# Second gate's row, e' group order, last q projection and third MLP pair's rows moved in a one-core attention and MLP block

## The chip, the cores and the metric

The kernel runs on one core of a Trainium2 chip. The metric is the time of one execution on the device in microseconds (us); lower is better. The engines are PE (matrix products, with weight loads PEld), DVE (vector), ACT (scalar), POOL (GpSimd) and SP (it issues DMAs; ACT and POOL issue some as well). They run in parallel, each through its own instructions in order.

## The reference

One transformer block on 2048 tokens of width 640 in float32. Both halves are modulated by a condition `c`.

```python
mod = (silu(c) @ w_mod).reshape(1, 6, 1, -1)
sa, ca, ga, sb, cb, gb = six rows of mod
h = layernorm(x) * (1 + ca) + sa
x = x + ga * A(h)          # linear attention, 32 heads of 20
h = layernorm(x) * (1 + cb) + sb
x = x + gb * B(h)          # (relu(h @ w1 + b1) ** 2) @ w2 + b2, 1728 hidden columns

# A: q, k, v = h @ wqkv; pq, pk = per-head products with w_phi
phi = concat(softmax(p), softmax(-p))
o   = phi_q @ (phi_k^T v) / (phi_q @ sum(phi_k) + 1e-6)
A   = o @ wo
```

## The kernel before

Tokens are taken in 16 tiles of 128 rows, or 8 pairs. Products are made in float32 by splitting each operand into a high and a low part (three products each: high-high, high-low, low-high; `mm(three(...))`, line 78). The low part is a subtraction on DVE (`lo`, line 88).

The first stage, to about 250 us, makes k and v for all tiles, q for most, and sums phi_k^T v in PSUM. In the same stage the modulation rows are made. The second gate (row 5 of `mod`) ends as a column form `MT[5]`, in a row buffer of the pool tag `s1`; `mod_sum(5, gate_b)` reduces it to `gate_b`, 128x5, on DVE (line 310). `spread_row` (lines 328, 329) then writes `gate_b` to DRAM as 640 single elements and reads it back broadcast to all 128 partitions as `gb_b`; both DMAs are on SP. The first gate is treated the same way earlier (`gate_a`, `ga_b`).

The second stage, from about 252 to 389 us, is written out by hand for PE, DVE, ACT and POOL (lines 768 to 1216); the order of SP's DMAs is left to the scheduler there. Its first lines project the last q tiles (`do_q`) and treat pair 0. Then a loop runs over the pairs, `for j in range(NB)`. For a tile t:

- `e_prod(t)` on DVE multiplies phi_q by the sum of phi_k (`scr`) and reduces by head (`dn`); POOL finishes the denominators; `e_recip` and `e_scale` on DVE give the scaled features `ezb` (e').
- `tr_e(j, groups)` transposes the scaled features of a pair on PE in six groups (`te`): groups 0 to 4 with four transposes, group 5 with two. Each group goes into one of three PSUM banks in turn and is evicted by ACT into an `ept` row (five buffers).
- `num(j)` makes the numerators (`numa`, `numb`, `numc`), groups 0 to 5 in order; `num_hi` evicts the high part on ACT (`ot`, line 950). `num_lo` makes the low part: for pairs 0 and 1 PE subtracts the high part in PSUM (line 961) and ACT copies (line 964); later DVE subtracts (`ot`, line 88).
- `do_wo` makes the product with `wo` (`pwo`); ACT evicts it to `at` (line 982, two buffers) and issues its store (line 984).

In pair j of the loop the groups for pair j+1 are transposed in two batches, at two of three places (`te(0)` behind the first product with `wo`, `te(1)` behind the second, `te(2)` behind the third). The last q tiles' feature chains (`q_chain`, `exps`, `q_sums`) are spread over pairs 1, 3 and 5. Pair 3 ends with `mod_sum` and `spread_row` of the second gate. Pair 5 makes the first pair's new residual rows (`add_x(0, 0, 1)`: x plus attention, stored to DRAM as X1) and `bb = b2s * gb_b`, where `b2s` is a row of `s1` that holds b2 on all partitions. `p_load`, `p_hi` and `p_lo` load and split the MLP's weight rows (row buffers of `s1`).

The third stage is the MLP, pair by pair: `up` (seven groups n of two 128-column pieces), relu on ACT (line 1250), square on DVE (line 1251), splits `ra` and `rs`, and the product with w2. From pair 2 on a scheme with fewer products is used, with sums of blocks of the hidden values (`sums`, line 1265) and prepared combinations of w2, which come from DRAM through four ring buffers (`ring_a`, `ring_b`, `ring_c`, fetched by POOL at line 1360 as soon as a buffer is free). Between the products, `layer(j+1, at)` prepares the next pair's layer norm: loads, `add_x` (line 1080, with the store of X1 at line 1081), the statistics (`ln_pieces`, ACT lines 1494 and 1499 and small steps on POOL) and the transposes. The dictionaries `LN_AT...` say at which half group each step stands; `LN_AT2` is for the pair prepared during pair 2, where SP's order is written by hand as well. `residual` loads the old X1 rows (`xr`).

Of the kernel before, what the change touches and what calls it, by code (L numbers as in the profile page):

```python
# [11 lines left out]
AF = mybir.ActivationFunctionType  # L12
ALU = mybir.AluOpType
AX = mybir.AxisListType

P = 128
# [35 lines left out]
def kernel(  # L52
# [64 lines left out]
    def row(tag, name):  # L117
        return (pc if tag in ("s3", "s4") else mem).tile([P, D], F32, tag=tag, name=name, bufs=BUFS[tag])
# [16 lines left out]
    def pj(name):  # L135
        return [psA.tile([P, 512], F32, tag="pj", name=f"{name}_{h}", bufs=4) for h in range(2)]
# [171 lines left out]
    def mod_sum(part, dest):  # L308
        with tc.issue_after(newest(ET_.DVE)):
            nc.vector.tensor_reduce(dest, MT[part].rearrange("p (a b) -> p a b", b=P), axis=AX.X, op=ALU.add)  # L310
# [16 lines left out]
    def spread_row(h, col, dest):  # L327
        nc.sync.dma_start(GD[h].rearrange("c p -> p c"), col)
        nc.sync.dma_start(dest, GD[h].rearrange("c p -> (c p)")[None, :].to_broadcast([P, D]))
# [64 lines left out]
        if more:  # L394
            mod_sum(*more)

    def proj(nm, t, between=None):
        p = pj(f"p{nm}{t}")
        j, i = divmod(t, 2)
        s = slice(i * P, (i + 1) * P)  # L400
        for h, (a, b) in enumerate(CUT):
            terms = []
            for d in range(NC):
                w = W[nm, d]
                terms += three(HT[j][:, d, 0, s], HT[j][:, d, 1, s], w[:, 0, a:b], w[:, 1, a:b])
            at, hook = 0, None
            if between and h == between[0]:
                at, hook = between[1:]
                mm(p[h][:, : b - a], terms[:at], last=False)
                hook()  # L410
            mm(p[h][:, : b - a], terms[at:], first=(at == 0))
        return p
# [43 lines left out]
    def do_q(t, between=None):  # L456
        q_out(t, proj("q", t, between=between))
# [45 lines left out]
            nc.gpsimd.dma_start(w[2 * n : m, 0], w[2 * n : m, 1])  # L503

    ga_b = row("s4", "ga_b")
    b2s = []

    def biases():
        b2s.append(row("s1", "b2s"))
        nc.sync.dma_start(b2s[0], bass.AP(tensor=b2.tensor, offset=b2.offset, ap=[[0, P], [1, D]]))  # L510

    GB = []

# [359 lines left out]
    def e_prod(t):  # L873
        if t >= NT:
            return
        z = SCR[t % 2]
        nc.vector.tensor_tensor(z, flat(ET[t]), flat(zb), op=ALU.mult)  # L877
        dn = DN[t] = small([P, 2, H], "dn", f"dn{t}", 3)
        nc.vector.tensor_reduce(dn.rearrange("p s h -> p (s h)"), heads(z), axis=AX.X, op=ALU.add)  # L879
        rs = rs_q[:, t].rearrange("p (s h) -> p s h", s=2)  # L880
        dd = DD[t] = small([P, H], "dd", f"dd{t}")
        nc.gpsimd.tensor_tensor(dd, rs[:, 0], rs[:, 1], op=ALU.mult)
        nc.gpsimd.tensor_scalar(dd, dd, 1e-6, None, op0=ALU.mult)
        for s in range(2):
            nc.gpsimd.tensor_tensor(dn[:, s], dn[:, s], rs[:, 1 - s], op=ALU.mult)  # L885
            nc.gpsimd.tensor_tensor(dd, dd, dn[:, s], op=ALU.add)
# [25 lines left out]
    def tr_e(j, gs):  # L912
        for g in gs:
            o, n = GR[g]
            p = bank(f"te{j}_{g}")
            t = EPT[j, g] = feat("s4", f"ept{j}_{g}")
            for i in range(2):
                for c in range(2 if g < 5 else 1):
                    a = c * 256 + i * P
                    b, m = (2 * o + 120 * c, 120) if g < 5 else (1200, 80)  # L920
                    nc.tensor.transpose(p[:m, a : a + P], EU[2 * j + i][:, b : b + m], ident)  # L921
            if g < 5:
                nc.scalar.activation(t[:120], p[:120].rearrange("p (s n) -> p s n", s=2), AF.Copy)
            else:
                nc.scalar.activation(t[:80, 0], p[:80, :256], AF.Copy)

    def num(j):
        OT[j] = ht(f"ot{j}", j)
        ps = [bank(f"numa{j}"), bank(f"numb{j}"), tp(f"numc{j}")]
        for g in range(5):  # L930
            for c in range(2):
                mm(ps[g // 2][64 * c : 64 * c + 64, (g % 2) * 256 : (g % 2) * 256 + 256],
                   [(kvd[:, g, 64 * c : 64 * c + 64], EPT[j, g][:120, c])], first=(g % 2 == 0), last=False, skip=True)
        for a, b in ((0, 64), (64, 120)):
            mm(ps[2][a:b, 256:], [(kv5[:, a:b], EPT[j, 5][:80, 0])], first=False, last=False, skip=True)
        NUM[j] = ps
        OT[j, 5] = row("s3", f"ot5_{j}")[:, 80:336].bitcast(F32R)
# [10 lines left out]
    def num_hi(j):  # L948
        for src, hi, _ in num_parts(j):
            nc.scalar.activation(hi, src, AF.Copy)  # L950

    def num_lo(j):

        if j >= DIRECT:
            for b, (src, hi, low) in enumerate(num_parts(j)):
                r = GR[5][1] if b == 3 else P
                lo(low[:r], src[:r], hi[:r])
            return
        for b, (src, hi, _) in enumerate(num_parts(j)):
            r = 120 if b == 3 else P  # L960
            nc.tensor.matmul(src, neg[:r, :r], hi, start=False, stop=True, skip_group_check=True)
        for b, (src, _, low) in enumerate(num_parts(j)):
            r = GR[5][1] if b == 3 else P
            nc.scalar.activation(low[:r], src[:r], AF.Copy)
# [70 lines left out]
    def p_load(n=1):  # L1035
        for _ in range(n):
            if todo["load"]:
                k, f = todo["load"].pop(0)
                prep_load(k, f, places[k, f](f"w{k}_{f}"))
# [76 lines left out]
    kv_masks()  # L1116
    e_prod(2)
    load_e(4)
    do_q(q0 + 3, (1, 8, lambda: tr_e(0, range(3))))
    tr_e(0, (5, 3, 4))  # L1120
    num(0)
    num_hi(0)
    num_lo(0)
    e_prod(3)
    e_recip(2)
    e_recip(3)
# [7 lines left out]
    for j in range(NB):  # L1134
        nxt = j + 1 < NB
        b, c = 2 * j + 5, 2 * j + 6
        te_at = (0, 1) if 0 < j < 6 else (1, 2)
        if j == 4:
            load_x1(0)
        if j < 5:  # L1140
            p_load()
        if j != 5:
            e_prod(b)
        e_recip(b - 1)
        e_scale(b - 1)
        if j == 5:
            q_chain(KEPT + 3, False)
            add_x(0, 0, 1)
            nc.vector.tensor_tensor(bb, b2s[0], gb_b, op=ALU.mult)
            ln0 = ln_parts(XM[0], "b0")  # L1150
        load_e(b + 2)
        def te(at):
            for i, gs in enumerate((range(3), (5, 3, 4))):
                if nxt and te_at[i] == at:
                    tr_e(j + 1, gs)

        do_wo(j, 0, 0)
        te(0)
        if j == 5:
            exps(EQ[KEPT + 3])  # L1160
            q_sums(KEPT + 3)
            e_prod(b)
        do_wo(j, 0, 1)
        if j == 7:
            t2(0, 0)
            t2(0, 1)
        te(1)
        if j == 5 or j == 6:
            next(ln0)
        if j in SUMS:  # L1170
            q_sums(KEPT + SUMS[j])
        e_prod(c)
        if j != 5:
            e_recip(b)
            e_scale(b)
        do_wo(j, 1, 0)
        if j == 7:
            t2(0, 2)
            t2(0, 3)
        te(2)  # L1180
        if nxt:
            num(j + 1)
            num_hi(j + 1)
        do_wo(j, 1, 1, 0, 8)
        if j == 7:
            t2(0, 4)
        if not nxt:
            do_wo(j, 1, 1, 8, 16)
        if nxt:
            do_wo(j, 1, 1, 8, 11)  # L1190
            num_lo(j + 1)
            do_wo(j, 1, 1, 11, 16)
        if j == 5:
            e_recip(b)
            e_scale(b)
        if j in SPREAD:
            q_chain(KEPT + SPREAD[j], False)
            exps(EQ[KEPT + SPREAD[j]])
        if j == 3:
            mod_sum(5, gate_b)  # L1200
            spread_row(1, gate_b, gb_b)
        load_e(c + 2)
        if j == 5:
            next(ln0)
        if 1 <= j < 6:
            p_hi()
        if j == 5:
            p_lo(4)
            p_load(4)
        if j == 6:  # L1210
            p_hi(4)
            p_lo(5)
            p_load(3)
        if j == 7:
            p_load(2)
    order.__exit__(None, None, None)

# [264 lines left out]

    LN_AT0 = {"load": 2, "xx": 3, "add": (5, 6), "ln": (5, 6, 7, 7, 8, 9), 10: (0, 1), 11: (2, 3), 12: (4,)}
    LN_AT1 = {"load": 3, "add": (5, 5), "ln": (5, 6, 6, 7, 8, 8), 9: (0, 1), 11: (2, 3), 12: (4,)}
    LN_AT2 = {"load": 0, "xx": 3, "add": (6, 6), "ln": (7, 7, 8, 8, 9, 9), 10: (0, 1), 11: (2, 3), 12: (4,)}
    LN_AT = {"load": 0, "add": (3, 4), "ln": (4, 5, 6, 6, 7, 7), 8: (0, 1), 10: (2, 3), 12: (4,)}
    PREPS = iter([1, 3] + [2, 1, 2, 2, 1, 2] + [1, 1] + [1, 2])

# [204 lines left out]
```

## Time and profile before

| | |
|---|---|
| Median of 3 runs | 768.94 us (768.92 to 770.37) |
| The profiled execution | 769.86 us |
| Its span, first to last instruction | 768.2 us |
| Mean granted PE clock | 1.000 |
| Busy: PE / DVE / ACT / POOL | 759.3 / 593.8 / 434.6 / 144.2 us |
| Moved by DMA | 126.69 MB, mean 165 GB/s |

A line of the timeline reads: start in us, length in us, engine, line of the kernel, operation, what it writes and reads by the program's names, shapes, how many were merged, and in brackets the idle time of the engine just before it with what ended that. `SPq`, `ACTq` are DMAs issued by these engines. A line of the windows reads: stretch, its length, then the busy time (and instructions) of PE, PEld, DVE, ACT and POOL, the granted clock, the busy share of the 16 DMA engines, and GB/s. Matmuls are pipelined and their ends are modelled, so PE counts as busy in some short waits.

### The profile page before, as it was taken

Reading aid. Unit: us, or ns where it says so; the run is one execution under the profiler, and the core shown is the slowest. Engines: PE = TensorE matmul, PEld = TensorE weight load, DVE = VectorE, ACT = ScalarE, POOL = GpSimd, SP = SyncE. Lnnn points to the kernel's source line nnn. Section 1 sums busy time; section 2 is a strip of 40 time slices with the busy share of each in tenths; the row PEclk is TensorE's granted clock in tenths of the full one; section 3 lists DMA queues with packets and bytes.
Section 4 is the critical chain, followed back from the end, with each engine's and each line's share of the span. In section 5 each row is a group of like instructions: output and inputs, shape, how many; then the busy total and the mean of one; then the engine's idle time right before and its main releaser. Section 6 shows DMA issues by size and latency. Waiting matters only on the chain.

```text
span 768.2 us, 15300 instructions
## 1 busy us (share of the span) xinstructions
PE 759.3 (99%) x5967; PEld 739.8 (96%) x5967; DVE 593.8 (77%) x1083; ACT 434.6 (57%) x971; POOL 144.2 (19%) x301
## 2 busy tenths in 40 slices
PE   9999999999999999999999999999999999999997
PEld 8999999999999989888999999999999999999996
DVE  6598897989999999999565667866767666675666
ACT  5766756767843454545776647465553636445331
POOL 3001101101100255442101000231321313222110
PEclk9999999999999999999999999999999999999999
DMA  9811431343333344155356367996766758766450
GB/s 327 305 65 73 137 103 54 104 139 114 119 104 109 117 142 170 70 80 160 107 180 222 110 226 253 286 323 195 226 181 197 232 177 262 221 184 192 130 165 35
DMA packets 52151, 126.69 MB, mean 165 GB/s; under 512 B 7335, under 2 KB 8103, under 8 KB 52079
## 3 DMA queue, kind: packets, MB, share of 16 engines
q1 hardware_dynamic: 34744, 84.65, 33.1%
q0 software_dynamic: 14752, 35.76, 16.7%
q10 hardware_dynamic: 2583, 5.30, 1.8%
q8 instruction: 47, 0.77, 0.4%
q14 instruction: 25, 0.20, 0.1%
HBM read 95.70 MB, written 29.89 MB: 163 GB/s over the span
## 4 chain that ended last, share of the span: by engine, by line
PE 85%; DVE 8%; issue 2%; DMA 2%; POOL 2%; ACT 1%; SPq 0%; POOLq 0%; DVEq 0%
PE up L78 23%; PE acc L78 17%; PE pk L78 9%; PE pv L78 9%; PE pq L78 8%; PE pwo L78 5%; PE acc3x L78 5%; PE kvp L450 3%; DVE dn L879 2%; DVE scr L877 2%; DVE ezb L901 1%; PE tb L357 1%; PE te L921 1%; DMA ring_b<-td_b 1%; PE ta L357 1%
## 5 line engine op out<-in xcount | busy, mean ns | idle before, releaser
L78 PE MATMUL up<-h,w 128*128 128x256 f32 x1640 | 206.4, 278 | 0.0
L78 PEld LDWEIGHTS up<-h,w 128*128 128x128 f32 x1640 | 196.1, 188 | 0.0
L1250 ACT ACTIVATE ft<-up,b_t 128x256 f32<-128x256 f32 x104 | 48.9, 470 | 115.1 <-PE up L78 114.6
L78 PE MATMUL acc<-w,ra 128*128 128x384 f32 x452 | 97.4, 335 | 0.0
L1251 DVE TENSOR_TENSOR ft<-ft 128x256 f32<-128x256 f32 x104 | 44.1, 424 | 51.2 <-ACT ft L1250 49.6
L78 PE MATMUL pwo<-wo,ot 128*128 128x256 f32 (+3 forms) x512 | 80.8, 312 | 0.6 <-DVE ot L88 0.6
L78 PEld LDWEIGHTS pwo<-wo,ot 128*128 128x128 f32 (+1 forms) x512 | 74.5, 188 | 3.8 <-issue 2.7
L78 PE MATMUL pq<-wq,hT 128*128 128x384 f32 (+1 forms) x480 | 75.2, 312 | 0.0
L78 PEld LDWEIGHTS acc<-w,ra 128*128 128x128 f32 x452 | 72.7, 188 | 0.7 <-DVE ra L88 0.5
L78 PE MATMUL pk<-wk,hT 128*128 128x384 f32 (+1 forms) x480 | 72.7, 308 | 0.0
L78 PE MATMUL pv<-wv,hT 128*128 128x384 f32 (+1 forms) x480 | 71.7, 307 | 0.0
L78 PEld LDWEIGHTS pq<-wq,hT 128*128 128x128 f32 x480 | 71.1, 188 | 0.6 <-issue 0.2
L78 PEld LDWEIGHTS pk<-wk,hT 128*128 128x128 f32 x480 | 70.5, 188 | 0.4 <-issue 0.2
L78 PEld LDWEIGHTS pv<-wv,hT 128*128 128x128 f32 x480 | 70.1, 188 | 0.0
L88 DVE TENSOR_TENSOR ra<-ft,ra 128x384 fp32r<-128x384 f32 (+2 forms) x86 | 36.8, 448 | 32.9 <-ACT ra L1274 20.2
L78 PE MATMUL acc3x<-w,ra 128*128 128x256 f32 x248 | 42.3, 278 | 1.4 <-DVE end L1418 1.4
L1360 POOL DMA_DIRECT2D ring_a<-td_a x34 | 18.3, 537 | 125.5 <-PE acc L78 103.2
L1274 ACT ACTIVATE ra<-ft 128x384 fp32r<-128x384 f32 x48 | 25.2, 526 | 28.4 <-DVE ft L1251 22.4
L78 PEld LDWEIGHTS acc3x<-w,ra 128*128 128x128 f32 x248 | 39.5, 188 | 1.8 <-DVE end L1418 1.6
L1265 DVE TENSOR_TENSOR ft<-ft 128x128 f32<-128x128 f32 x136 | 33.3, 286 | 1.2
L441 DVE TENSOR_REDUCE sk<-ek 128x64 f32<-128x1280 f32 x16 | 23.7, 1484 | 12.4 <-ACT ek L436 10.8
L885 POOL TENSOR_TENSOR dn<-dn,rs_q 128x32 f32<-128x32 f32 x32 | 20.1, 629 | 68.1 <-DVE dn L879 67.8
(264 smaller groups left out, 1406.5 us busy)
## 6 DMA issues: line engine op xcount, KB each, us to landing
ring_c<-td_c POOLq DMA_DIRECT2D x34, 384.0 KB, 4.0
ring_a<-td_a POOLq DMA_DIRECT2D x34, 384.0 KB, 4.1
ring_b<-td_b POOLq DMA_DIRECT2D x34, 256.0 KB, 4.0
esp<-eq SPq DMA_DIRECT2D x12, 640.0 KB, 3.2
el<-esp SPq DMA_DIRECT2D x12, 640.0 KB, 4.0
rw<-in_w SPq DMA_DIRECT2D x23, 320.0 KB, 3.1
wm<-in_w_mod SPq DMA_DIRECT2D x20, 320.0 KB, 3.7
xb<-in_x SPq DMA_DIRECT2D x8, 640.0 KB, 4.0
```

The source lines that it names most:

```text
L78: nc.tensor.matmul(o, a, b, start=first and i == 0, stop=last and i == len(terms) - 1, skip_group_check=skip,)
L88: (eng or nc.vector).tensor_tensor(out_lo, full, hi.bitcast(F32), op=ALU.subtract)
L357: nc.tensor.transpose(p[:, i * P : (i + 1) * P], xn[:, i, d * P : (d + 1) * P], ident)
L441: nc.vector.tensor_reduce(s, heads(flat(e)), axis=AX.X, op=ALU.add)
L450: nc.tensor.matmul(kvp[g // 4][64 * c : 64 * c + 64, a : a + 2 * n].rearrange("p (s n) -> p s n", s=2), v[:, u], e[:, :, o : o + n], start ...
L877: nc.vector.tensor_tensor(z, flat(ET[t]), flat(zb), op=ALU.mult)
L885: nc.gpsimd.tensor_tensor(dn[:, s], dn[:, s], rs[:, 1 - s], op=ALU.mult)
L1250: nc.scalar.activation(r, p, AF.Relu, bias=b1_t[:, f : f + 1])
L1251: nc.vector.tensor_tensor(r, r, r, op=ALU.mult)
L1265: nc.vector.tensor_tensor(t[:, o], t[:, a], t[:, b], op=op)
L1274: nc.scalar.activation(a[:, 0, :3], t[:, :3], AF.Copy)
L1360: nc.gpsimd.dma_start(RING[j, n, r], TD[n][r].bitcast(F32R))
```

## The change

Four edits. First, `mod_sum` and `spread_row` of the second gate move from the end of pair 3 to pair 5, behind `add_x`; b2 is read straight into `bb`; the product `bb * gb_b` is made in place at the end of pair 7. Second, for the pairs whose batches stand at places 0 and 1 (the transposes for pairs 2 to 6), the second batch goes in the order 3, 4, 5 instead of 5, 3, 4. Third, the projection of the last q tile is cut: its first half is evicted at once (`pq_out(0)`), the transposes and numerators of pair 0 come behind 8 of the 15 products of its second half, the other 7 products behind the numerators and their first evictions, and the second half is evicted behind `num_lo(0)`. Fourth, in `LN_AT2` the second `add_x` moves from half group 6 to half group 7.

```diff
-    def proj(nm, t, between=None):
-        p = pj(f"p{nm}{t}")
+    def proj(nm, t, between=None, p=None):
+        p = p or pj(f"p{nm}{t}")
...
     ga_b = row("s4", "ga_b")
-    b2s = []
-
+    
     def biases():
-        b2s.append(row("s1", "b2s"))
-        nc.sync.dma_start(b2s[0], bass.AP(tensor=b2.tensor, offset=b2.offset, ap=[[0, P], [1, D]]))
+        nc.sync.dma_start(bb, bass.AP(tensor=b2.tensor, offset=b2.offset, ap=[[0, P], [1, D]]))
...
     load_e(4)
-    do_q(q0 + 3, (1, 8, lambda: tr_e(0, range(3))))
-    tr_e(0, (5, 3, 4))
-    num(0)
-    num_hi(0)
+    PQ[q0 + 3], pq = EQ[q0 + 3][:, 0], pj("pq_last")
+
+    def pq_out(h):
+        nc.scalar.activation(PQ[q0 + 3][:, slice(*CUT[h])], pq[h][:, : CUT[h][1] - CUT[h][0]], AF.Copy)
+
+    def inside():
+        pq_out(0)
+        tr_e(0, range(3))
+        tr_e(0, (5, 3, 4))
+        num(0)
+        num_hi(0)
+
+    proj("q", q0 + 3, (1, 8, inside), pq)
     num_lo(0)
+    pq_out(1)
     e_prod(3)
...
             add_x(0, 0, 1)
-            nc.vector.tensor_tensor(bb, b2s[0], gb_b, op=ALU.mult)
+            mod_sum(5, gate_b)
+            spread_row(1, gate_b, gb_b)
             ln0 = ln_parts(XM[0], "b0")
         load_e(b + 2)
         def te(at):
-            for i, gs in enumerate((range(3), (5, 3, 4))):
+            for i, gs in enumerate((range(3), (3, 4, 5) if te_at[0] == 0 else (5, 3, 4))):
                 if nxt and te_at[i] == at:
                     tr_e(j + 1, gs)
...
-        if j == 3:
-            mod_sum(5, gate_b)
-            spread_row(1, gate_b, gb_b)
         load_e(c + 2)
...
         if j == 7:
+            nc.vector.tensor_tensor(bb, bb, gb_b, op=ALU.mult)
             p_load(2)
...
-    LN_AT2 = {"load": 0, "xx": 3, "add": (6, 6), "ln": (7, 7, 8, 8, 9, 9), 10: (0, 1), 11: (2, 3), 12: (4,)}
+    LN_AT2 = {"load": 0, "xx": 3, "add": (6, 7), "ln": (7, 7, 8, 8, 9, 9), 10: (0, 1), 11: (2, 3), 12: (4,)}
```

## The prediction

> **What bounds the kernel now.** I read the page first, then what the matrix engine waited for, then the timeline around each of those waits.
>
> ```profile
> span 768.2 us, 15300 instructions
> PE 759.3 (99%) x5967; PEld 739.8 (96%) x5967; DVE 593.8 (77%) x1083; ACT 434.6 (57%) x971; POOL 144.2 (19%) x301
> ```
>
> PE is busy 759.3 of 768.2 us and the granted clock is full, so no edit here can win more than the time in which PE stands still. The waits of PE (us in total, times, longest) say where that is:
>
> ```profile
> PE acc L78 <- DMA ring_b<-td_b: 0.7, 1, 0.7
> PE pwo L78 <- DVE ot L88: 0.6, 1, 0.6
> PE te L921 <- ACT ept L923: 0.3, 1, 0.3
> ```
>
> Three places are within reach of this change: one wait for a ring transfer, one for DVE's `ot`, one for ACT's `ept`. Together the rows show 1.6 us of 768.9 (0.21%), and a little more in the weight loads that stop with them. About 0.2%, 1.5 us, is what a measurement of this kernel can tell from no change, so the question is whether all three go and nothing new comes.
>
> **The last q behind the numerators.** The edit adds no work; it moves seven 256-column products of `pq` between the evictions of the first numerators and the products that subtract them, where PE waits today:
>
> ```profile
> 272.06 0.19 PEld L961 LDWEIGHTS numa<-ot,neg 128*128 128x128 f32 x1 [0.39 <-ACT ot L950]
> 272.89 0.29 PEld L961 LDWEIGHTS numc<-ot,neg 128*128 128x128 f32 x2 [0.53 <-ACT ot L950]
> 277.28 0.23 DVE L906 TENSOR_TENSOR ezb<-el,dn 128x80 f32<-128x80 f32 x1
> 277.80 1.33 PEld L921 LDWEIGHTS te<-ident,ezb 128*120 128x120 f32 x12
> 254.00:308.00 54.00, 53.91 (x399) 49.03 (x399) 51.87 (x74) 25.78 (x62) 25.58 (x54) 1.00 0.47 151
> 306.91 0.74 ACT L436 ACTIVATE eq<-eq 128x640 f32<-128x640 f32 x1 [2.99 <-DVE eq L433]
> 309.82 1.63 PE L921 MATMUL te<-ident,ezb 128*80 128x128 f32 x10 [0.33 <-ACT ept L923]
> ```
>
> It fills up to 0.39+0.53 = 0.9 us. But the next transposes, at 277.80, need `ezb` of tile 3, which DVE ends at 277.51; so at most 0.3 us is carried on. And DVE is busy 51.87 of the 54 us to 308, waiting for neither PE nor ACT after 254; at 306.91 ACT waits for DVE, and at 309.82 PE waits for ACT. What PE wins before 309 it loses there. I book nothing; the bounds are -0.3 us and, since 0.33 us of waiting covers a delay, nothing on the other side. `pq_out(1)` comes later on ACT, with no reader until pair 5.
>
> **The order of the e' groups.** Same 10 transposes, same evictions; group 5 (two transposes) goes last instead of first in the second batch, for the numerators of pairs 2 to 6. Each transpose group needs the bank that ACT frees from the first batch.
>
> ```profile
> 309.18 1.56 ACT L923 ACTIVATE ept<-te 120x512 f32<-120x512 f32 x3
> 355.31 1.25 PE L921 MATMUL te<-ident,ezb 128*80 128x128 f32 x10
> 331.19 0.69 DVE L88 TENSOR_TENSOR ot<-numa,ot 128x512 fp32r<-128x512 f32 x1 [0.42 <-ACT ot L950]
> ```
>
> ACT frees one bank about every 0.5 us (1.56 for three). Two transposes cover half of that, four nearly all. The batch takes 1.63 us at 309.82 and 1.25 at 355.31, where nothing holds it: 0.38 us are lost, 0.2 of them between the groups. I take -0.2 us (bounds -0.38 and 0). It is carried on, since at 331.19 DVE waits for what PE has made. In the other pairs the batch is not held. The eviction that waits for the first numerators is now the short one, which ACT likes and PE does not notice.
>
> **The gate's row.** In pair 3 DVE loses the sum for `gate_b`. In pair 5 it gains that sum and loses the `bb` product; in pair 7 it gains the product.
>
> ```profile
> 336.37 0.81 DVE L310 TENSOR_REDUCE gate_b<-mt 128x5 f32<-128x640 f32 x1
> 337.10 1.48 DVE L877 TENSOR_TENSOR scr<-eq,zb 128x1280 f32<-128x1280 f32 x1
> 349.55 2.71 PE L78 MATMUL pwo<-wo,ot 128*128 128x384 f32 x14 [0.57 <-DVE ot L88]
> 357.50 0.82 DVE L1149 TENSOR_TENSOR bb<-b2s,gb_b 128x640 f32<-128x640 f32 x1
> 391.42 0.42 DVE L1251 TENSOR_TENSOR ft<-ft 128x256 f32<-128x256 f32 x1 [1.10 <-ACT ft L1250]
> ```
>
> The next DVE instruction starts 0.73 us after the sum did, and from there DVE runs without a break to the `ot` for which PE waits 0.57 us; PE also starts up again after a wait, which the row does not count. Taking 0.73 off DVE ends that wait: I take -0.7 us (bounds -0.57 and -0.73). In pair 5 a sum of 0.81 replaces a product of 0.82: nothing. In pair 7 the product falls into the 1.10 us in which DVE waits for the first relu of the MLP: nothing, unless `gb_b` is not there. `b2` going straight into `bb` frees one row of `s1`, so later weight rows can only load earlier.
>
> What moves with the sum is its two DMAs on SP: `gate_b` out to DRAM and back to all partitions.
>
> ```profile
> 337.21 0.38 SPq L328 DMA_DIRECT2D gate<-gate_b  x1
> 348.77 0.33 SPq L329 DMA_DIRECT2D gb_b<-gate  x1
> 144.03 0.38 SPq L328 DMA_DIRECT2D gate<-gate_a  x1
> 153.96 0.34 SPq L329 DMA_DIRECT2D ga_b<-gate  x1
> 357.81 0.33 ACTq L984 DMA_DIRECT2D a<-at  x1
> 367.27 0.47 ACT L982 ACTIVATE at<-pwo 128x384 f32<-128x384 f32 x1
> 367.27:373.68 6.41, 6.41 (x51) 6.35 (x50) 2.77 (x4) 4.80 (x11) 2.01 (x2) 1.00 0.61 202
> 373.91 1.08 PE L78 MATMUL numa<-ept,kvd 120*64 120x256 f32 x8
> ```
>
> The write has 2.5 KB, yet SP could issue the read only 11.6 us later (9.9 us for the first gate). On SP that is harmless: the rows behind it serve pair 6 and later, `gb_b` lands by about 375 and is used at 390. But in its new place, at 358.3 (357.50+0.82; times here on the clock of before), it follows 0.5 us behind the store of `at`. `at` has two buffers, so that store must have landed when ACT writes the next but one `at`, at 367.27; behind that wait on ACT stand the `ept` evictions that PE needs at 373.91. ACT has 4.80 us of work between, so a landing up to 373.91-4.80 = 369.1 costs PE nothing. If the write holds up the store as it held SP, the landing is 358.3+9.9 = 368.2 (free) to 358.3+11.6 = 369.9 (0.8 us). The upper bound is the store that followed the write in pair 3: its buffer was needed 15.1 us after the write, unnoticed, which would be 373.4 here, or 4.3 us. I take nothing, since the store is issued ahead of the write.
>
> Here the Trainium skill weighs in, on its page "DMA: Bandwidth & Descriptors". Its section "Anatomy of one DMA" gives a DMA on GpSimd's path about 2 us and its bytes over 436 GB/s, by which an estimate for the write is 2 us, and its place would not matter; the trace's 11.6 us, on SP's path, says otherwise. Its section "Queues, rings and completion order" says that the completion count of a DMA lands only after every earlier write of that DMA engine, of other queues too. That speaks against this change: the store could not be reported as landed before the write is, and the time would be the first rival's below. No row of before shows it alone.
>
> **The third pair's rows.** `add_x` of tile 1 moves from behind the first product of group 3 of pair 2 to behind its second, with its store, and SP's loads of `xr` behind it in a hand-written order.
>
> ```profile
> 506.25 1.55 DVE L1080 TENSOR_TENSOR xm<-xm,xx 128x640 f32<-128x640 f32 x2
> 507.09 1.05 SPq L1081 DMA_DIRECT2D x<-xm  x2
> 508.15 0.54 POOL L1360 DMA_DIRECT2D ring_b<-td_b  x1 [1.68 <-PE acc L78]
> 508.20 2.10 SPq L1405 DMA_DIRECT2D xr<-x  x2
> 502.00:518.00 16.00, 15.32 (x121) 15.12 (x120) 10.33 (x27) 10.38 (x23) 5.62 (x12) 1.00 1.01 325
> 515.61 0.41 PEld L78 LDWEIGHTS acc<-ring_b,rs 128*128 128x128 f32 x3 [0.88 <-DMA ring_b<-td_b]
> DMA to landing us min/median/max: 3.0/4.7/7.4
> 509.27 1.01 DVE L1265 TENSOR_TENSOR ft<-ft 128x128 f32<-128x128 f32 x4
> 509.39 0.73 ACT L1494 ACTIVATE xx<-xm 128x640 f32<-128x640 f32 x1
> 510.57 0.47 ACT L1250 ACTIVATE ft<-up,b_t 128x256 f32<-128x256 f32 x1 [0.36 <-PE up L78]
> 513.57 0.68 PE L78 MATMUL acc<-ring_a,rs 128*128 128x384 f32 x3
> 514.91 0.63 POOL L1360 DMA_DIRECT2D ring_b<-td_b  x1 [0.16 <-issue]
> ```
>
> The DMA engines are full (1.01) for 16 us at 325 GB/s. The transfer of `ring_b` issued at 508.15 took the 7.4 us and PE waited 0.88 for it. One store and two loads of 320 KB, together 0.98 MB or 3.0 us at 325 GB/s, now come about 3 us later: the add stands behind the sums, 509.27+1.01 = 510.3, and ends at 511.1. `ring_b` needs to gain 0.88 of those 3.0, and PE goes on at 515.61-0.88 = 514.73. I take -0.88 us (bounds -0.88 and 0).
>
> The cost: ACT's statistic of tile 1 (509.39) waits for that add until 511.1, and behind it on ACT stands the relu at 510.57, then the split of `rs`. They come 1.3 us later, and the split ends near 513.5; PE takes it at 513.57, the low half two products later. Cost 0, at most 0.3 us. On POOL the statistics' small steps come later too, and behind them the fetch at 514.91, at about 516; its rows are needed one group (508.15 to 514.91, 6.8 us) after 514.73, at 521.5, which leaves it 5.5 us against the median of 4.7.
>
> **Sum.** -0.2-0.7-0.88 = -1.8 us. The profiled execution took 769.86 us for its span of 768.2, so 768.1 for a span of 766.4. The runs' median is 768.94, 0.92 below it; taking the 1.8 off that gives 767.2. This assumes that the median run has the same three waits, though the ring's may be part of the 0.92.
>
> **Rivals.**
> - The write holds the store of `at`, landing near 370: 0.8 to 1.2 us of the gain go, 768.2. For it: SP's 11.6 us. Against it: 9.9 for the first gate.
> - The ring's wait stays, or is not there in runs without a profile: -0.9 alone, 768.0. For it: the 0.92 us; the engines are full as before.
> - Slower: the same write, but the store held as long as the unseen bound allows. From a landing at 369.1+1.8+1.5 = 372.4, 14.1 us after its issue, it outweighs all gains by 0.2%; at 373.4 with the ring's wait kept the time is 768.94-0.9+4.3 = 772.3, at the middle, 372.9, 770.9 or more. The next store, at 364.63, would queue behind it.
> - More than forecast: the 0.3 us of the last q and the 0.38 of the groups carry on: 768.94-0.3-0.38-0.73-0.88 = 766.7. For it: the waits near 272 are real. Against it: DVE has no pause to 308.
>
> **How the numbers follow.** Forecast 0.45, with 0.37 of it beyond 0.2% (767.4) and the rest just short; the held store 0.17; the kept ring wait 0.14; slower 0.15; more 0.09. So faster 0.46, same 0.37, slower 0.17. The range runs from 766.4, the best case and 0.3 for the spread of executions, to 769.3, the first two rivals together (769.0) and the same 0.3; it leaves out the slower case, 0.15.
>
> **What would show it.** Right: no wait of `pwo` for DVE `ot` near 348, none for `ring_b` near 513, the batch at 309 near 1.4 us, the matrix engine's waits for `ot` L950 near 272 gone but its wait near 309 longer. Wrong: a long idle time of ACT before an `at` near 366 that no PE product ends, and PE waiting for an `ept` near 373; a wait for another ring near 520; DVE waiting for `gb_b` before the product of pair 7.

## The result, and the profile after

The changed kernel is slower, by 0.2%. Its median was 770.76 us (769.58 to 773.29, 22 runs) beside 769.61 us (768.76 to 770.69, 22 runs) for the kernel before on the same chip: a ratio of 1.0021, 95% interval 1.0015 to 1.0027. The profiled execution took 770.9 us with a span of 769.2, 1.0 us more than before, at full granted clock.

The waits of PE (us in total, times, longest) after the change:

```profile
PE numa L78 <- ACT ept L923: 1.6, 1, 1.6
PE acc3x L78 <- DVE end L1425: 1.4, 1, 1.4
...
PE te L919 <- ACT ept L921: 0.4, 1, 0.4
PE up L78 <- ACT ft L1257: 0.3, 1, 0.3
```

Two of the three waits that the prediction meant to remove are gone from these rows (`ring_b`, and DVE's `ot`); a wait for `ept` of 1.6 us and one for a relu have come. (The 1.4 us for `end` is in the last pair and was there before.) Subtracting the start of every PE product before from the start of the same product after gives a running shift; the steps in it are what the change did. It stands at -0.3 us from the first products on (no edit is behind that), at -0.5 at 315, at -0.3 again at 330, at -1.0 at 352, then at **+1.2 at 375**, +1.4 at 505, +0.9 at 520 and +1.0 at the end. The edits had won 0.7 us by 372, and one event at 374 took 2.2.

That place in the timeline of the changed kernel (start, length, engine, line, operation, and in brackets the idle time before and what ended it), ACT and DMA issues first, then PE and its weight loads:

```profile
356.80 0.33 ACTq L982 DMA_DIRECT2D a<-at  x1
357.32 0.37 SPq L328 DMA_DIRECT2D gate<-gate_b  x1
...
366.20 0.47 ACT L980 ACTIVATE at<-pwo 128x384 f32<-128x384 f32 x1
...
369.88 0.32 SPq L329 DMA_DIRECT2D gb_b<-gate  x1
...
370.39 0.39 ACT L980 ACTIVATE at<-pwo 128x256 f32<-128x256 f32 x1 [3.72 <-PE te L919]
...
367.55 1.47 PE L919 MATMUL te<-ident,ezb 128*120 128x128 f32 x12
368.78 3.07 PE L78 MATMUL pwo<-wo,ot 128*128 128x384 f32 x16
371.84 1.63 PE L919 MATMUL te<-ident,ezb 128*80 128x128 f32 x10
375.06 1.08 PE L78 MATMUL numa<-ept,kvd 120*64 120x256 f32 x8 [1.59 <-ACT ept L923]
...
375.06 0.63 PEld L78 LDWEIGHTS numa<-ept,kvd 120*64 120x64 f32 x8 [1.83 <-ACT ept L923]
```

The write of the gate follows the store of `at` by 0.52 us, and SP can issue the read only 12.6 us later, as feared. But the store was not held: by the semaphore events of the trace it had landed 2.7 us behind the write's issue, while the counts of the write itself came from 11.1 us on; and the eviction of `at` at 366.20, which needs that store landed, starts without any idle time. What ACT waits 3.72 us for, at 370.39, is PE. And PE was not late with its work: the `pwo` products end at 367.71, and PE goes straight on. Before the change the same eviction waited 1.09 us:

```profile
367.27 0.47 ACT L982 ACTIVATE at<-pwo 128x384 f32<-128x384 f32 x1
368.83 0.39 ACT L982 ACTIVATE at<-pwo 128x256 f32<-128x256 f32 x1 [1.09 <-PE pwo L78]
369.62 1.58 ACT L923 ACTIVATE ept<-te 120x512 f32<-120x512 f32 x3 [0.40 <-PE te L921]
```

The bracket in the row at 370.39 names `te`, since that is the last product that ended ahead of the release; the missing 2 us show only in the semaphore events of the trace. PE raises one count with its products, and other engines wait for values of it. End of the product, and the time at which the count rose, changed kernel:

```
product ends  365.88   367.71   368.15   368.59   369.03   371.85
count rises   365.89   370.37   370.43   370.49   370.55   371.86
```

Four counts come 1.5 to 2.7 us late, then all within 0.2 us, like a backlog that is let go. ACT starts 0.02 us after the first. Call this **late counts**. The trace's DMA packets show what else happened there: PE's own instructions arrive in transfers of 16 KB, one for every 256 of its 12,038 recorded instructions (5967 products, as many loads, and 104 semaphore steps); the one that began at 366.51 before the change began at 368.86 after it and landed at 370.28. Undisturbed transfers begin, at the earliest, when PE has started some 155 instructions past a multiple of 256; by that count (called due, below) it fell due at 363.1, 5.8 us after the write. All of the core's DMAs together moved 373 GB/s from 357.3 to 359.3, but 18, 86 and 19 GB/s in the three stretches of 2 us from 361.3 to 367.3. So the first theory was: the write of 640 elements stops the DMA engines for some 10 us (the **stop** from here on), PE's instruction transfer falls due in that stop, and until it has landed PE's counts come late.

### The profile page after: what moved, and what is told of

It is laid out like the page before. It is cut to its first block, busy times and chain, and to the rows that moved or that the text cites. A ratio compares the mean times of both kernels' runs of the same rounds, so it can differ in the third digit from the quotient of the medians.

```text
span 769.2 us, 15303 instructions
## 1 busy us (share of the span) xinstructions
PE 760.1 (99%) x5967; PEld 740.0 (96%) x5967; DVE 594.3 (77%) x1083; ACT 436.6 (57%) x971; POOL 144.6 (19%) x301
## 4 chain that ended last, share of the span: by engine, by line
PE 88%; DVE 8%; POOL 1%; DMA 1%; ACT 1%; issue 1%; DVEq 0%; ACTq 0%; POOLq 0%
PE up L78 24%; PE acc L78 18%; PE pk L78 9%; PE pv L78 9%; PE pq L78 8%; PE pwo L78 5%; PE acc3x L78 5%; PE kvp L450 3%; DVE dn L877 2%; DVE scr L875 2%; DVE ezb L899 1%; PE tb L357 1%; DMA a<-at 1%; PE te L919 1%; PE foldk L280 1%; PE ta L357 1%
## 5 line engine op out<-in xcount | busy, mean ns | idle before, releaser
L78 PE MATMUL pq<-wq,hT 128*128 128x384 f32 (+1 forms) x450 | 70.7, 312 | 0.0
L78 PEld LDWEIGHTS pq<-wq,hT 128*128 128x128 f32 x450 | 66.7, 188 | 0.6 <-issue 0.2
L441 DVE TENSOR_REDUCE sk<-ek 128x64 f32<-128x1280 f32 x16 | 23.7, 1484 | 12.4 <-ACT ek L436 10.9
```

The costliest lines, as they stand in the source:

```text
L78: nc.tensor.matmul(o, a, b, start=first and i == 0, stop=last and i == len(terms) - 1, skip_group_check=skip,)
L441: nc.vector.tensor_reduce(s, heads(flat(e)), axis=AX.X, op=ALU.add)
```

## The experiments

**Is it the gate's row?** `gate_only` is the kernel before with that edit alone (below); `no_gate` is the changed kernel with the same lines turned back.

```diff
             add_x(0, 0, 1)
-            nc.vector.tensor_tensor(bb, b2s[0], gb_b, op=ALU.mult)
+            mod_sum(5, gate_b)
+            spread_row(1, gate_b, gb_b)
...
-        if j == 3:
-            mod_sum(5, gate_b)
-            spread_row(1, gate_b, gb_b)
...
         if j == 7:
+            nc.vector.tensor_tensor(bb, bb, gb_b, op=ALU.mult)
```

> The kernel before with the gate edit alone. Theory (late signals): the 640-element write, issued near 358, stops the DMA queues for 10 to 12 us; PE's own instruction transfer, due near 365, falls into that stop, and until it has landed the ends of PE's products near 368 are reported late, so ACT stands idle about 3.7 us ahead of an `at` near 366 to 370 and PE stands 1.6 us or more ahead of `numa` near 374. Sum: -0.7 at 349 as predicted, +2.2 at 374, so about +1.5 us against the kernel before (ratio 1.002). Rival (the loss comes from another edit, or from all together): -0.7 us, and no idle ACT near 368.

> The changed kernel with the gate's row left where it was (the other three edits stay). Theory: no late signal near 368; -0.2 us from the e' groups and -0.3 from the third pair's rows (its ring wait of 0.88 gone, a wait of 0.6 for the relu come), so about -0.5 us against the kernel before (ratio 0.9993). Rival (another edit is the loss): +0.5 us or more.

Measured: `gate_only` 769.70 us against 769.58, ratio 1.0006 (0.9997 to 1.0015); `no_gate` 769.36, ratio 1.0000 (0.9991 to 1.0009). In the profile of `gate_only` PE wins 0.7 us at 349.55 and loses 1.56 at 374. The rows of ACT's timeline and of PE's waits are those of the changed kernel:

```profile
369.79 0.39 ACT L980 ACTIVATE at<-pwo 128x256 f32<-128x256 f32 x1 [3.08 <-PE te L919]
```

```profile
PE numa L78 <- ACT ept L923: 1.5, 1, 1.5
```

Four late counts, by 0.9 to 2.0 us. In `no_gate` there are none and the eviction waits 1.09 us as before. The event at 374 belongs to the gate's row. But `gate_only` alone is not clearly slower than before, let alone by the 1.5 us that were expected. Its 11 executions spread from 768.4 to 771.7, and the profiled one, 770.35, lies above the median: the lateness may differ from one execution to the next, which one profile can't show.

**Is it the write, or the sum's place on DVE?** `gate_rows` keeps the place and writes 128 pieces of 20 bytes instead of 640 of 4 (it leaves out putting the entries of `gb_b` back into order); `gate_pair4` keeps the pieces and puts the step at the end of pair 4.

```diff
# gate_rows, for the second gate
-        nc.sync.dma_start(GD[h].rearrange("c p -> p c"), col)
+        nc.sync.dma_start(GD[h].rearrange("c p -> (c p)").rearrange("(p c) -> p c", c=NC), col)
# gate_pair4
             add_x(0, 0, 1)
-            mod_sum(5, gate_b)
-            spread_row(1, gate_b, gb_b)
...
+        if j == 4:
+            mod_sum(5, gate_b)
+            spread_row(1, gate_b, gb_b)
         load_e(c + 2)
```

> The changed kernel, with the second gate written as 128 pieces of 20 bytes instead of 640 of 4 bytes (this leaves the entries of `gb_b` in another order). Theory, with the stop priced by the piece: the write takes a fifth, 2 to 2.5 us, SP can issue the read about 2.5 us after the write, PE's transfer near 365 is not held, no late signal: about -1.3 us against the kernel before (ratio 0.9983). If the stop were a fixed price of any such write: as the changed kernel, +1.2 us. Rival (the loss is not the write's but the sum's place on DVE): as the changed kernel, +1.2 us, with the read issued early all the same.

> The changed kernel with the sum for `gate_b` and its two DMAs at the end of pair 4 instead of in pair 5, about 7 us earlier; the rest as changed. Theory: the write is issued near 351, its stop ends near 363, and PE's instruction transfers near 347.5 and 365.4 lie on both sides of it; no late signal, the gain of about 1 us up to 372 is kept and the third pair adds 0.3: about -1.3 us against the kernel before (ratio 0.9983). Should the transfer fall into the stop all the same, a wait of ACT for PE shows just there. Rival (any write behind pair 3 delays the kernel, since the stores of `at` stand in the same queues): a wait again near the first `at` behind the write, +1 us or so.

Measured: `gate_rows` 768.73 us, ratio 0.9991 (0.9983 to 1.0000); `gate_pair4` 769.01, ratio 0.9992 (0.9983 to 1.0001). No late counts in either; the gain is about half of the 0.17% that was expected. SP's two issues, first of `gate_rows`, then of `gate_pair4`:

```profile
357.46 0.32 SPq L329 DMA_DIRECT2D gate<-gate_b  x1
360.10 0.32 SPq L332 DMA_DIRECT2D gb_b<-gate  x1
```

```profile
351.04 0.38 SPq L328 DMA_DIRECT2D gate<-gate_b  x1
360.96 0.33 SPq L329 DMA_DIRECT2D gb_b<-gate  x1
```

The same 2.5 KB hold SP for 2.6 us as 128 pieces and for 9.9 as 640: the price goes with the number of pieces, not with the bytes. With 128 pieces the sum in pair 5 does what the prediction said: PE's shift goes from -0.17 at 330 to -0.90 at 352, and there is no step at 374. So it is the write. `rows_view` does the same with nothing left out, the readers taking `gb_b` through a strided view:

```diff
+    gb_c = gb_b.rearrange("q (p c) -> q c p", p=P)
...
-        nc.vector.tensor_tensor(o, a, gb_b[:, c], op=ALU.mult)
+        nc.vector.tensor_tensor(by_col(o), by_col(a), gb_c[:, c.start // P : c.stop // P], op=ALU.mult)
```

> The changed kernel with the second gate written as 128 pieces of 20 bytes, and the three readers of `gb_b` (`bb`, `by_gate`) reading it through a strided view, so that nothing is left out. Theory: as the run with 128 pieces, -1 to -1.3 us against before (ratio 0.9985), if DVE reads the strided view at the same rate (0.82 us for 128x640, 0.5 for 128x384); if it reads it at half rate, every product with the gate is 0.4 to 0.8 us longer, beside PE except at the end of the last pair, where it costs 0.5 to 1 us. Rival to the theory: the loss of 2.2 us at 374 again.

769.70 us, ratio 1.0011 (1.0002 to 1.0020), a miss: the strided product costs 1.45 us on DVE where the plain one costs 0.82, and PE's shift, -0.94 at 362, is down to -0.35 at 760.

```profile
389.33 1.45 DVE L1224 TENSOR_TENSOR bb<-bb,gb_b 128x640 f32<-128x640 f32 x1
```

**Is it PE's instruction transfer?** Tiny extra products at the start move PE's transfers earlier against the work; everything else stays. They cost 4.6 to 14.9 us ahead of 24 us, so only the later steps of the profile are read.

```diff
+    for i in range(29):        # 12 in after_shift2, 14 in before_shift14, 35 in pair4_shift35
+        nc.tensor.matmul(warm[:, :32], ones, ones[:, :32], start=True, stop=True)
```

> The changed kernel with 29 tiny extra products (128x32) behind the warm-up at the start, so that PE's instruction transfers, one for every 256 of its instructions, come some 8 us earlier against the work; the write of the gate stays where it is. Theory (PE's completion counts are late while its next instruction transfer is held by the write): the transfer due at 365.5 now comes near 357.5, before the stop begins, and the next one near 374, behind it; no late count near 368, ACT idle 1.1 us instead of 3.7 ahead of the second `at`, no wait of `numa` near 374. Time: about 2 us less than the changed kernel from that place, or -1 us against the kernel before, plus what the extra products cost at the start (0 to 1 us). Rival (the write's stop itself holds PE's counts, at whatever time the transfer is due): the late counts near 368 and the 3.7 us stay.

> The changed kernel with 12 of the tiny products instead of 29, so that PE's instruction transfer due near 365.5 comes some 3 us earlier against the work: still inside the stop (359.5 to 370), as is the short one (8 KB, of another engine) due near 365.6. Theory A (late counts need a transfer of PE's instructions that falls due in the stop, wherever in it): late counts and the loss of 2 us at 374 stay. Theory B (it takes both transfers falling due together at the stop's end): late counts gone or short, the loss gone, as with 29.

> The kernel before with the same 29 extra products. Theory: the transfer seen at 348.4, just behind the stop of the write at 337.2 (338 to 349), is now due near 340.5, inside it; it is held to 349 or so, and PE's completion counts from about 341 to 350 come late, so ACT or DVE, and after them PE, wait there though the order of the work is that of before: 1 to 4 us slower than before at that place. Rival (the write's stop itself, or the new place of the work): no late counts, the kernel before plus 0 to 1 us.

In `after_shift` PE's shift against the changed kernel falls from 10.9 to 8.7 us at 375: the 2.2 us are back, though the write and the work are where they were and SP's read still follows 12.05 us behind the write.

```profile
378.91 0.38 ACT L982 ACTIVATE at<-pwo 128x256 f32<-128x256 f32 x1 [1.33 <-PE pwo L78]
```

In `after_shift2`, with the transfer due 2.7 us after the write, three counts are late by 0.4 to 1.1 us and some 0.6 us are lost. But `before_shift` speaks against the theory: PE's transfer was due 1.4 us after the write in pair 3 and held until 11.6, and no count was late. The 0 to 1 us expected for the products was wrong, and the times of these runs (779.52, 771.93 and 783.61 us) are mostly theirs.

A second transfer, of 8 KB and of another engine, was held near 366 to 369 as well. Forty tiny instructions of ACT, or of DVE, at the start move that engine's transfers:

```diff
# after_act; after_dve the same with nc.vector.tensor_tensor(pad, ones[:, :48], ones[:, :48], op=ALU.add)
+    for i in range(40):
+        nc.scalar.activation(pad, ones[:, :48], AF.Copy)
```

> The changed kernel with 40 tiny extra ACT instructions at the start, which moves ACT's instruction transfers (8 KB for every 128 instructions) some 20 us earlier; PE's stay where they are. If the short transfer held near 366 to 369 is ACT's, it leaves the stop. Theory A (PE's own transfer is enough): late counts and the loss of 2 us at 374 stay. Theory B (the other engine's transfer takes part): they go.

> The same with 40 tiny extra DVE instructions. If the short transfer held near 366 to 369 is DVE's, it leaves the stop. Theory A: late counts and the loss of 2 us at 374 stay. Theory B: they go here and not with the ACT instructions, or the other way round, whichever engine's transfer it is.

In `after_act` the 8 KB transfer leaves the stop (353.6, write at 368.7): it is ACT's. Late counts stay in both, four each, by 0.6 to 1.7 and 1.0 to 2.1 us. The idle time of ACT in `after_act`:

```profile
380.83 0.38 ACT L982 ACTIVATE at<-pwo 128x256 f32<-128x256 f32 x1 [2.81 <-PE te L921]
```

So ACT's transfer is not needed for it. (Their times, 781.25 and 780.46 us, are the cost of the extra instructions.)

**Is the transfer enough, or does the place count too?** `before_shift14` and `pair4_shift35` put PE's transfer into the stops of pairs 3 and 4; `end5_stat` keeps the write in pair 5 but at the end of the pair, with the transfer outside, and with the mended statistic told of below; `sum_first` takes the stores of x out of the queues ahead of the write.

```diff
# end5_stat, against gate_pair4 (and the other ln of gate4_stat, below)
-        if j == 4:
+        if j == 5:
             mod_sum(5, gate_b)
             spread_row(1, gate_b, gb_b)
         load_e(c + 2)
# sum_first, against the changed kernel
-            add_x(0, 0, 1)
             mod_sum(5, gate_b)
             spread_row(1, gate_b, gb_b)
+            add_x(0, 0, 1)
```

> The kernel before with 14 tiny products at the start, so that PE's instruction transfer that fell due 9.3 us after the gate's write now falls due some 5.5 us after it, as in the changed kernel; all work in the order of before. Theory A (what counts is when PE's instruction transfer falls due in the write's stop): PE's completion counts 9.4 and 11.4 us after the write come late by 1 to 2.5 us, for the first time in pair 3. Theory P (the place in pair 5 is what counts): none late.

> The run with the gate's write at the end of pair 4, with 35 tiny products at the start, so that PE's instruction transfer due 14.5 us after the write now falls due about 6 us after it. Theory A: late counts 9 to 12 us after the write, and PE loses 0.5 to 2 us near there. Theory P: none, as without the products.

> The run with the gate's write at the end of pair 4 and the later statistic, but with the write at the end of pair 5, near 366, about 9 us behind its place in the changed kernel. PE's instruction transfer falls due near 365.4, just ahead of the stop, and the next one near 382, behind it. Theory A: no late counts, about -1.1 us against the kernel before (ratio 0.9986). Theory P: late counts 9 to 12 us after the write, near 375 to 378, and 1 to 2 us more.

> The changed kernel with the sum and the gate's two DMAs ahead of the first pair's new rows in pair 5 instead of behind them: the write is issued near 356 instead of 357.3, and ahead of the two stores of x (640 KB together) instead of behind them. PE's instruction transfer still falls due in the stop, some 7 us after the write. If the late counts need full DMA queues ahead of the write as well as that transfer: none late, about -1.3 us against the kernel before (ratio 0.9983). If the transfer and the place in pair 5 are enough: late counts 9 to 12 us after the write and +1 us, as in the changed kernel; the stores of x wait behind the write either way, and their next reader is far behind.

Worked out from the trace's transfers and semaphore events, one profiled execution of each kernel, all times in us behind the issue of the gate's write:

```
kernel          write in     PE's transfer due / began / landed   counts late by
after           pair 5       +5.8 / +11.5 / +12.9                 1.5 to 2.7 (4)
gate_only       pair 5       +5.8 / +10.6 / +11.7                 0.9 to 2.0 (4)
after_act       pair 5       +5.8 / +10.6 / +13.0                 0.6 to 1.7 (4)
after_dve       pair 5       +5.8 / +12.3 / +13.4                 1.0 to 2.1 (4)
after_shift2    pair 5       +2.7 /  +3.5 / +10.4                 0.4 to 1.1 (3)
after_shift     pair 5       began 1.8 ahead of the write         0.25 (1)
end5_stat       pair 5, end  began 0.9 ahead of the write         none
sum_first       pair 5       +7.3 / +11.2 / +12.1                 none
before          pair 3       +9.3 / +11.2 / +12.9                 none
before_shift14  pair 3       +5.6 / +10.7 / +12.2                 none
before_shift    pair 3       +1.4 / +11.6 / +12.6                 none
pair4_shift35   pair 4       +3.4 /  +8.4 / +11.8                 none
gate_pair4      pair 4       began 4.5 ahead of the write         none
```

`before_shift14` and `pair4_shift35` make no late counts: the theory that a held transfer is enough has fallen. (`before_shift14` took 773.82 us and `pair4_shift35` 784.70, of which the products are 4.6 and 13.9.) What stands: with the write behind the stores in pair 5, counts were late by more than 0.3 us in all five kernels whose PE transfer fell due in the stop, and by no more than 0.25 in `after_shift`, where it began ahead of the write. The stop of the first gate, near 144 to 154, agrees: where PE's transfer falls due in it, 5 of 15 kernels have counts late by 0.3 to 1.5 us (the kernel before one of 0.46, unnoticed; in 3 others a count has no record there); where the products made it due ahead of the write, none of 3. In no profile is a recorded count more than 0.2 us late outside the stops of the two writes.

But the landing of the transfer is not what lets the counts go. In `after_act` they rose from 12.1 us behind the write, ahead of its landing at 13.0, and in `after_dve` likewise. At the first gate, in `after_shift2` and in `before_shift14`, products that ended 9.3 us behind the write still had late counts, though the transfer had landed at 6.9.

`sum_first` takes away one thing that pair 5 has, 640 KB of stores in the queues ahead of the write: no recorded count is late, though the transfer is held. Two counts, of products that ended 9.9 and 10.0 us behind the write, have no record there, so this is weaker than it looks. And at the first gate no store stands right ahead of the write (the last DMA issued is a load of x, 3.3 us earlier), and counts were late all the same: such stores are no general condition. The time of `sum_first` is no better, though (770.45 us, ratio 1.0021, 1.0010 to 1.0033), and the reason is a surprise, the prediction's own rival:

```profile
355.62 0.38 SPq L328 DMA_DIRECT2D gate<-gate_b  x1
...
356.56 0.36 ACTq L982 DMA_DIRECT2D a<-at  x1
...
369.28 0.76 ACT L980 ACTIVATE at<-pwo 128x384 f32<-128x384 f32 x2 [3.23 <-DMA a<-at]
```

Here the store of `at` is issued 0.94 us behind the write instead of 0.52 ahead of it, and ACT waits 3.23 us for it, to 13.7 us behind the write. PE loses 1.7 us at 374. The write was issued 1.7 us earlier and costs PE about the same, by another wait.

**The third pair, and a better version.** `third_only` is the kernel before with that edit; `gate4_stat` is `gate_pair4` with the second statistic one half group later.

```diff
# third_only, in LN_AT2 of the kernel before
-"add": (6, 6)
+"add": (6, 7)
# gate4_stat, in LN_AT2 of gate_pair4
-"ln": (7, 7, 8, 8, 9, 9)
+"ln": (7, 8, 8, 8, 9, 9)
```

> The kernel before with the edit of the third pair's rows alone. Prediction on record: -0.9 us (ring wait of 0.88 gone, relu late at no more than 0.3). From the trace of the changed kernel: PE waits 0.3 us and its weight loads 0.6 for the relu of group 3, so -0.3 us net (ratio 0.9996), which is inside the noise; the trace must show the ring's wait gone and the relu's wait come. Rival (the ring's wait was already gone in runs without a profile): +0.5 us.

> The run with the gate's write at the end of pair 4, and in the third pair ACT's statistic of tile 1 one half group later (entries of ln 7, 8, 8, 8, 9, 9), so that the relu no longer stands behind it. Theory: -0.6 us as that run measured in its profile, and PE's wait of 0.3 us (0.6 of its weight loads) for the relu near 512 gone: about -1.1 us against the kernel before (ratio 0.9986). If the statistic's later steps come late for the transposes of the next pair, a new wait near 520 gives it back.

`third_only`: 769.40 us against 769.08, ratio 1.0003 (0.9994 to 1.0012). Its profile shows the ring's wait gone and this in its place (DVE, ACT, PE and its loads); PE's shift falls by 0.49 us net, from +0.14 at 505 to -0.35 at 520:

```profile
510.35 0.82 DVE L1080 TENSOR_TENSOR xm<-xm,xx 128x640 f32<-128x640 f32 x1
...
511.20 0.74 ACT L1494 ACTIVATE xx<-xm 128x640 f32<-128x640 f32 x1 [1.57 <-DVE xm L1080]
511.94 0.45 ACT L1250 ACTIVATE ft<-up,b_t 128x256 f32<-128x256 f32 x1
...
512.44 1.99 PE L78 MATMUL up<-h,w 128*128 128x256 f32 x15 [0.27 <-ACT ft L1250]
...
512.44 1.79 PEld L78 LDWEIGHTS up<-h,w 128*128 128x128 f32 x15 [0.59 <-ACT ft L1250]
```

With the statistic behind the relu (`gate4_stat`: 768.74 us against 769.35, ratio 0.9989, 0.9980 to 0.9998) and the write at the end of pair 5 (`end5_stat`: **768.48 us against 769.48, ratio 0.9987, 0.9978 to 0.9996**) the time lies below that of the kernel before, by 0.13%, and the ratio below the changed kernel's 1.0021. The rows of `end5_stat`, with the relu ahead of the statistic and one smaller wait for the next relu:

```profile
510.06 0.47 ACT L1258 ACTIVATE ft<-up,b_t 128x256 f32<-128x256 f32 x1 [1.08 <-PE up L78]
510.95 0.72 ACT L1502 ACTIVATE xx<-xm 128x640 f32<-128x640 f32 x1
...
514.91 1.98 PE L78 MATMUL up<-h,w 128*128 128x256 f32 x15 [0.15 <-ACT ft L1258]
```

## Why the prediction was wrong

The forecast was 767.2 us, 1.8 below the kernel before, with a range up to 769.3; the time was 770.76. The terms for the last q and for the sum on DVE came out as booked, the gains of the groups and of the third pair smaller, and the gate's write, put at nothing, took more than the others had won.

**The last q behind the numerators** (nothing): right. The waits of PE for `ot` near 272 are gone (its weight loads have a new one of 0.18 us, for ACT's copy), and PE's shift in `no_gate` is +0.05 us at 250, +0.13 at 274 and +0.07 at 308.

**The order of the e' groups** (-0.2): right in size, wrong in what follows. The batch at 309 takes 1.39 us instead of 1.63 and PE gains 0.2 to 0.24 us there. (The batch at 339 shrank as well, from 1.36 to 1.26, though the prediction had it as not held.) The prediction let that be carried on because at 331 DVE waits for PE. It is given back ten us later, at the next place where PE waits for DVE (before, then after):

```profile
319.25 0.83 PEld L78 LDWEIGHTS pwo<-wo,ot 128*128 128x128 f32 x5 [0.18 <-DVE ot L88]
```

```profile
318.99 1.18 PEld L78 LDWEIGHTS pwo<-wo,ot 128*128 128x128 f32 x7 [0.41 <-DVE ot L88]
```

The row with 0.18 was in the trace of before; the prediction left it out.

**The gate's row on DVE** (-0.7): right: -0.73 in the changed kernel and in `gate_rows` (330 to 352), -0.68 in `gate_only`. The wait itself has not ended, though: PE's weight loads wait 0.34 us for `ot` at 348.54, instead of 0.89 at 349.55. The product in pair 7 was free, as booked:

```profile
391.38 0.82 DVE L1221 TENSOR_TENSOR bb<-bb,gb_b 128x640 f32<-128x640 f32 x1
392.57 0.42 DVE L1258 TENSOR_TENSOR ft<-ft 128x256 f32<-128x256 f32 x1 [0.38 <-ACT ft L1257]
```

**The gate's write** ("I take nothing, since the store is issued ahead of the write"): this is the step that failed. The reason given was true, since the store landed in time; but it stood for all that the write could hold, so that the term for the write was put at nothing. The cost was +2.2 us, and what was held was not the store but PE's counts: the first count that ACT waited for came 2.7 us late, and PE then waited for ACT's `ept`. That the cost lies inside the bounds of 0 to 4.3 and at the place named (ACT's `at` near 366, PE's `ept` near 374) is luck, since the bounds and the place were worked out for a held store. What the prediction let the write hold were SP's loads and ACT's stores, not the engines' own instructions and not PE's counts. Its sign for being wrong, "a long idle time of ACT before an `at` near 366 that no PE product ends", would have missed it too: the bracket names a PE product. The argument from the page was misapplied as well. The Trainium skill's page "DMA: Bandwidth & Descriptors", section "Queues, rings and completion order", says that a completion count lands only after the earlier writes of the same DMA engine, whatever their queue; the prediction let this hold a store that stands ahead of the write. `sum_first` has the rival's held store, issued behind the write: the write's counts came until 9.8 us behind its issue and the store's until 13.3, 1.7 us longer than the 11.6 that SP had shown. That agrees with the page, though the run doesn't tell a held count from bytes that wait their turn.

**The third pair's rows** (-0.88, cost at most 0.3): the gain was right, the ring's wait of 0.88 is gone; the cost was mis-sized: PE's shift steps up by 0.56 us at the next `up` instead of 0 to 0.3 (net -0.49 in `third_only`, -0.48 in the changed kernel). The prediction counted how late the split of `rs` would be for its product and left out the next `up`, for which PE waits until the relu has read its bank (0.27 us, 0.59 of the weight loads, in `third_only`).

**The sum**: -0.3 at the start, about 0 from the last q and the groups, -0.7, +2.2, +0.25 in small steps up to 505, and -0.5 make +0.95, beside +1.0 of the span. Without the gate's row the three other edits give nothing that a measurement of 0.2% can tell (`no_gate`). The chances were added up loosely: those listed for the forecast and the rivals make 0.39 for same and 0.15 for slower, not 0.37 and 0.17; nothing else hangs on that.

**What stays open.** That the 640-piece write makes the counts late is shown: at the same place 128 pieces make none late. Why they are late is not settled. In pair 5 they were late by more than 0.3 us only where PE's instruction transfer fell due in the stop; elsewhere that was not enough, and its landing doesn't end the lateness. Stores ahead of the write may matter in pair 5, on one run with two counts missing, but not at the first gate. Nor do the two halves add up: `gate_only` (1.0006) and `no_gate` (1.0000) leave 0.0015 of the 1.0021. A lateness that differs between executions would explain it; no run shows that.

## What to carry to other kernels

A DMA of 640 pieces of 4 bytes is to be counted as some 10 us in which whatever travels by DMA behind it may be held, the engines' instructions included, and in which PE's counts can come late. It is to be placed where nothing on the critical path is due in that time, or cut into fewer pieces (128 instead of 640 made it 2.6 us). A short wait that is removed is worth only the way to the next place where the same engine waits for the same partner, so look there before booking it. When an engine waits long for products that ended early, compare the ends with the semaphore events before naming a cause.

## What the runs showed of the hardware

- PE's completion counts can rise up to 2.7 us after the products' ends, while PE goes on working; four of them then come within 0.2 us (the changed kernel).
- PE's instructions come in 16 KB for every 256 of them, those of ACT in 8 KB (`after_act`); a transfer held for 10 us (`before_shift`: due +1.4, began +11.6) did not make PE stand.
- 640 elements of 4 bytes keep SP from the dependent read for 9.4 to 12.6 us (both gates, all kernels), 128 pieces of 20 bytes for 2.6 (`gate_rows`).
- A store issued 0.5 us ahead of that write landed 2.7 us behind its issue (the changed kernel), one issued 0.9 us behind it landed at 13.3 (`sum_first`).
- A 128x640 product on DVE with one operand at a stride of 5 elements took 1.45 us instead of 0.82 (`rows_view`).
